# One group's query load, three range checks and a split projection: three moves in the instruction order of a fused linear-attention and SoLU kernel

## The chip, the cores and the metric

The kernel runs on one core of one Trainium2 chip. The metric is device time in microseconds for one launch, lower is better. Three runs of the kernel before are given: 374.28, 375.96 and 377.16 us, median 375.96 us. A further execution was taken with the profiler.

## The reference

A gated linear attention with a per-channel decay is followed by a feed-forward block with a SoLU activation and a layer norm. The attention inputs come as float32, the two weight matrices as float64, and all arithmetic on the chip is float32.

```python
# attention: B, H, S, D = 4, 8, 768, 48; alpha in 0.8 .. 1.0
for t in range(S):
    state = alpha[:, :, t, :, None] * state + k_t (outer) v_t
    y[:, :, t] = q_t @ state
x = y.transpose(0, 2, 1, 3).reshape(B * S, H * D)      # 3072 x 384
h = x @ w_in                                           # 384 -> 1024
solu = h * softmax(h)
ln = (solu - mean(solu)) / sqrt(var(solu) + 1e-6) * g_ln
out = ln @ w_out                                       # 1024 -> 384
```

## The kernel before, in words

The 768 time steps are cut into G = 6 groups of 128. A group holds the 128 steps of all four batches, so the feed-forward block sees 512 token columns per group. For each group the attention part does this:

- `load` brings alpha (`an`), keys (`kn`) and queries (`qn`) from HBM, four requests each on SyncE's queue (SP), one per batch; `load_v` does the same for the values. A queue issues in program order, and a request that has to wait holds up all requests behind it.
- `alpha_T` turns alpha on VectorE, `scan_back` and `scan_on` run the running products of the decay along time on VectorE (L204, three parts each: heads 0 to 3, heads 4 to 7, and the last 16 channels of all heads).
- Keys and queries are multiplied by these products into `kT`, `qv` and `qe`. For group 1 TensorE turns them first (`turned`, L164, tiles `tp_k`, `tp_q`), and VectorE multiplies straight out of PSUM: L779 for the keys, L794 and L802 for the queries.
- `move_lasts` (eight requests, L232) and `move_firsts` (four requests, L237) copy the finished queries within SBUF, from `qe` and `qv` into `q64` (the tile `lot`), which lays two batches on top of each other. These are requests on the same SP queue.
- `scores` (L278) multiplies keys and queries into four PSUM banks `a0` to `a3`, `masked` (L289, VectorE) cuts the upper triangle into `sT`.
- `decay` (L261, GpSimd) multiplies the running `state` by the group's whole decay, which it reads out of the last column of `q64`; then `read_state` (L333, `y<-lot,state`) and `read_values` (L333, `y<-sT,vn`) give the attention output. ScalarE copies it to `x` (L363).
- `up` (L394) gives h in two PSUM buffers `h`; `down` (L507) multiplies the activations by `w_out`. It accumulates eight matmuls in a PSUM buffer `o` per batch, `down(n, half)` giving four of them; a third argument picks some of those four.

Group 0 is special: the weights arrive as float64 words and are rebuilt as float32 on VectorE (`bits`, L612 to L624) while `up` of group 0 runs. `in_range(i)` goes with it: on ScalarE it squares the high words of weight piece i (L598) and takes an exponential of the squares (L601), each with an accumulator read behind it, to find out whether the fast path holds. `alpha_over` (L196) checks the range of alpha in the same manner. The results of both are looked at only at the end of the kernel. `in_range` and `alpha_over` share one scratch tile `sq`. Pieces 5, 6 and 7 lie in slots 1 to 3 of `room`, and the activations of group 1 are written over these slots later.

`mean(0)` sums the columns of `w_out` on TensorE (L645) and ScalarE copies the sums to `o_mean` (L650); `mean(1)` spreads them over the partitions by a matmul (L652) and ScalarE copies that to `mean_sb` (L653). `hold` (L516) copies a finished projection out of PSUM. `finish` does the normalization of one batch and sends it out.

Where the order is written out by hand (the stretch between the end of group 0's `up` and the start of group 1's `up`), each engine executes its instructions in the order of the Python calls. A wait is a semaphore wait at the head of an engine's instruction. This is the stretch that the change touches, from 54 to 104 us of the profile. From group 1's `up` on, the attention of group g+1 is spread over the eight `up` steps of group g by the tables `first` and `usual`; in both tables the queries' load stands behind `move_firsts`.

Of the kernel before, what the change touches and what calls it, by code (L numbers as in the profile page):

```python
# [32 lines left out]
def fast_path(ctx, tc, q, k, v, alpha, moe_w_in, moe_w_out, moe_g_ln, out):  # L33
# [66 lines left out]
    qn = const.tile([P, H, TQ, D], FP, name="qn")  # L100
# [30 lines left out]
    def load(src, dst, g):  # L131
        t = slice(g * P, (g + 1) * P)
        for b in range(B):
            nc.sync.dma_start(
                out=dst[32 * b : 32 * b + 32].rearrange("t h u d -> t h (u d)"),
                in_=src[b, :, t, :].rearrange("h (t u) d -> t h (u d)", u=TQ),
            )
# [20 lines left out]
    def turned(src, ends, out, blocks=range(NB)):  # L158

        x = by_token(src)  # L160
        for j in blocks:
            for b in range(B):
                cols = x[:, b, j, 0:E0] if j < H else ends[:, b, E0 * (j - H) : E0 * (j - H) + E0]
                nc.tensor.matmul(  # L164
                    out[j // NP][32 * b : 32 * b + 32, j % NP], lhsT=cols, rhs=ident, start=True, stop=True,
                    tile_position=(0, 32 * b), skip_group_check=True,
                )
# [10 lines left out]
    def firsts(src, dst):  # L178
        nc.vector.transpose(out=dst.rearrange("p h (t u) -> p h u t", u=TQ), in_=src[:, :, :, 0:E0])  # L179

    def lasts(src, dst):
        nc.vector.transpose(
            out=dst.rearrange("p j (i t u) -> p u j i t", u=TQ, i=2),
            in_=src[:, :, :, E0:D].rearrange("p (j i) u d -> p u j i d", i=2),
        )

    def alpha_T(g):
        nc.gpsimd.memset(aT[:, :, 0:1], 0.0)
        firsts(an, aT[:, 0:H, 1:SW])
        lasts(an, aT[:, H:NB, 1:SW])  # L190

    def alpha_over(g):
        x = an.rearrange("p h u d -> p (h u d)")
        sq = one.tile([P, 768], FP, name="sq").bitcast(U8)[:, 0 : x.shape[1]]
        for i, sign in enumerate((1.0, -1.0)):
            nc.scalar.activation(  # L196
                out=sq, in_=x, func=AF.Relu, scale=sign, bias=mone, accum_out=over[:, g, i : i + 1]
            )
# [28 lines left out]
    def move_lasts():  # L227

        for b in range(B):
            i, c = divmod(b, 2)  # L230
            for k in range(2):
                nc.sync.dma_start(out=q64[64 * i + E0 : 64 * i + 64, c, k::2], in_=qe[32 * b : 32 * b + 32])  # L232

    def move_firsts():
        for b in range(B):
            i, c = divmod(b, 2)
            nc.sync.dma_start(out=q64[64 * i : 64 * i + E0, c], in_=qv[32 * b : 32 * b + 32, 0:H])  # L237
# [27 lines left out]
    def quarter(b):  # L265
        return slice(32 * b, 32 * b + 32)
# [4 lines left out]
    def scores(g, half, a=None):  # L271
        a = a or banks("a", [NP, P])
        for last in range(2):
            for i in (0, 2, 1, 3):
                h = half * NP + i
                kb, qb = (H + h // 2, H + h) if last else (h, h)
                for b in range(B):
                    nc.tensor.matmul(  # L278
                        a[b][:, i], lhsT=kT[quarter(b), kb], rhs=qv[quarter(b), qb, 0:P], start=not last and not i, stop=bool(last),
                        tile_position=(32 * b, 0), skip_group_check=True,  # L280
                    )
        masks[half] = a
# [3 lines left out]
    def masked(half, batches=range(B)):  # L286
        a = masks[half]
        for b in batches:
            nc.vector.tensor_tensor(  # L289
                out=sT[:, b, half * NP : half * NP + NP], in0=a[b], in1=mask[:, None, :].to_broadcast([P, NP, P]),  # L290
                op=ALU.mult,
            )
# [90 lines left out]
    def u_of(g, f):  # L383
        return slots[((0, 5, 4), (1, 2, 3))[g % 2][f // 3]][:, T4 * (f % 3) : T4 * (f % 3) + T4]
# [116 lines left out]
    def down(n, half, part=range(HF)):  # L501
        g, b = divmod(n, B)
        d = st[n]
        if half == 0 and 0 in part:
            d["o"] = ps_o.tile([P, 512], FP, tag="o", name="o")
        for f in (half * HF + i for i in part):
            nc.tensor.matmul(  # L507
                d["o"][:, 0 : DM + 1], lhsT=u_of(g, f)[:, b * P : b * P + P], rhs=w_out[:, f], start=(f == 0),
                stop=(f == FC - 1), skip_group_check=True,
            )  # L510

    def hold(n):

        a = 2 * H * SW + (DM + 1) * (n % 2)
        st[n]["held"] = lot[:, a : a + DM + 1]
        nc.scalar.copy(out=st[n]["held"], in_=st[n]["o"][:, 0 : DM + 1])  # L516
# [73 lines left out]
    def in_range(i, parts=(0, 1)):  # L590


        if not float64:
            return
        if 0 in parts:
            hi = raws[i][:, :, :, 1].bitcast(FP)
            squares[i] = one.tile([P, F], FP, name="sq").rearrange("p (c f) -> p c f", c=hi.shape[1])
            nc.scalar.activation(out=squares[i], in_=hi, func=AF.Square, accum_out=far[:, i, 0:1])  # L598
        if 1 in parts:
            sq = squares.pop(i)  # L600
            nc.scalar.activation(out=sq, in_=sq, func=AF.Exp, scale=-(2.0**24), accum_out=far[:, i, 1:2])  # L601
# [36 lines left out]
    def mean(half):  # L638


        m = ps_h.tile([P, 512], FP, tag="h", name="sums")[:, 0:DM]
        if half == 0:
            for f in range(FC):
                r = quarter(f % 4)
                nc.tensor.matmul(  # L645
                    m[r], lhsT=ones[:, 0:32], rhs=w_out[:, f, 0:DM], start=f < 4, stop=f >= FC - 4,
                    tile_position=(0, r.start), skip_group_check=True,
                )
            made["m"] = work.tile([P, DM], FP, name="o_mean")
            nc.scalar.mul(out=made["m"], in_=m, mul=-1.0 / (32 * DFF))  # L650
        else:
            nc.tensor.matmul(m, lhsT=ones, rhs=made["m"], start=True, stop=True)  # L652
            nc.scalar.copy(out=mean_sb, in_=m)  # L653
# [117 lines left out]
    scaled(7)  # L771
    tq = three("tp_q", [(ps_a, "a0"), (ps_a, "a1")])
    turned(qn, ends_q, tq, range(H))
    in_range(5)
    in_range(6)
    for i in range(3):
        scan_back(1, i)
        part = slice(NP * i, NP * i + NP)
        nc.vector.tensor_tensor(out=kT[:, part], in0=tk[i], in1=hk[:, part], op=ALU.mult)  # L779
    inverses(1)  # L780
    mean(0)
    down(0, 1)
    mean(1)
    hold(0)
    alpha_over(1)
    load(alpha, an, 2)
    tq += three("tp_q2", [(ps_h, "h")])
    turned(qn, ends_q, tq, range(H, NB))
    load(q, qn, 2)
    down(1, 1)  # L790
    hold(1)
    keys_back(1, three("tp", [(ps_a, "a2"), (ps_a, "a3"), (ps_h, "h")]))
# [2 lines left out]
    apart()  # L795
    ends_of_decay()
    move_lasts()
    in_range(7)
    for i in range(2):
        scan_on(1, i)  # L800
        part = slice(NP * i, NP * i + NP)
        nc.vector.tensor_tensor(out=qv[:, part, 0:P], in0=tq[i], in1=aT[:, part, 1:SW], op=ALU.mult)  # L802
    move_firsts()
    down(2, 0)
    scores(1, 0)
    decay(1)
    masked(0)
    alpha_T(2)
    down(2, 1)
    scores(1, 1)  # L810
    masked(1)
# [592 lines left out]
def kernel(tc, *args):  # L1404

    with ExitStack() as ctx:
        taken = fast_path(ctx, tc, *args)
    with tc.If(taken > 0):
        general_path(tc, *args)
# [30 lines left out]
```

## Time and profile before

| what | value |
|---|---|
| median of three runs | 375.96 us (374.28 to 377.16) |
| the profiled execution | 377.03 us |
| its span, first to last instruction | 375.2 us, so 1.83 us lie around it |
| mean granted TensorE clock | 0.995 of full |
| TensorE (PE) busy | 362.3 us, 97% of the span |
| VectorE (DVE) busy | 246.8 us, 66% |
| ScalarE (ACT) busy | 147.0 us, 39% |
| GpSimd (POOL) busy | 125.4 us, 33% |

Each row of the timeline gives the start in us, the length in us, engine, line, operation, the tile written and the tiles read, the size, the number of instructions and, in brackets, the idle time before the first of them with what ended it. Rows of matmuls come in pairs per matmul for float32. TensorE's busy time counts matmuls whose ends are modelled, so 97% says how little it waits, not how well it is used.

The stretches around the change, by busy time of each engine (us in ten us):

| window us | PE | DVE | ACT | POOL | clock |
|---|---|---|---|---|---|
| 60 to 70 | 9.43 | 9.69 | 4.91 | 0.00 | 1.00 |
| 70 to 80 | 8.77 | 9.66 | 8.62 | 0.47 | 1.00 |
| 80 to 90 | 9.52 | 8.00 | 2.09 | 0.00 | 1.00 |
| 90 to 100 | 8.10 | 9.13 | 1.75 | 4.25 | 0.83 |
| 100 to 110 | 10.00 | 9.84 | 7.01 | 4.80 | 1.00 |

### The profile page before, as it was taken

To read this page: it belongs to the slowest core of one execution; us is meant where nothing else is said; L and a number is where in the kernel's file an instruction comes from. 1 tells how busy PE (TensorE), PEld (TensorE's weight loads), DVE (VectorE), ACT (ScalarE), POOL (GpSimd) and SP (SyncE) were. 2 spreads that over 40 slices of the span, in tenths; PEclk is the share of its full clock that TensorE was granted. 3 is DMA by queue.
4 is the path that set the end of the run, shared out by engine and by line. 5 is a ranking of instruction groups with operands and counts; after the bars stand their busy time and mean duration, and the time that the engine had idled before them with its cause. 6 is when DMAs were issued, how large, how long until landed. Compare 5 with 4: busy or idle time off the path is not lost. (4 is left out here: it accounts for less than half of the span.)

```text
span 375.2 us, 10040 instructions
## 1 busy us (share of the span) xinstructions
PE 362.3 (97%) x4341; PEld 216.4 (58%) x4341; DVE 246.8 (66%) x375; ACT 147.0 (39%) x260; POOL 125.4 (33%) x129
## 2 busy tenths in 40 slices
PE   8989999898999999999999999999999999999994
PEld 8775355464755565556575556575555565555652
DVE  1997979979988978954756954756955224544500
ACT  3649853870366253351532251532241231332100
POOL 7020000002347892664112664113673211333200
PEclk9999999999899999999999999999999999999999
DMA  9996986076158706554035354005041000000011
GB/s 179 180 328 158 202 275 134 0 159 124 66 119 178 166 17 132 124 127 113 23 87 106 84 134 107 24 3 107 14 108 35 24 23 0 24 22 21 24 45 49
DMA packets 72871, 36.06 MB, mean 96 GB/s; under 512 B 48232, under 2 KB 70000, under 8 KB 72816
## 3 DMA queue, kind: packets, MB, share of 16 engines
q1 hardware_dynamic: 71792, 34.39, 38.8%
q10 hardware_dynamic: 1024, 0.92, 0.7%
q8 instruction: 36, 0.59, 0.7%
q14 instruction: 19, 0.16, 0.1%
HBM read 25.30 MB, written 4.72 MB: 80 GB/s over the span
## 5 line engine op out<-in xcount | busy, mean ns | idle before, releaser
L507 PE MATMUL o<-w_out,room 128*128 128x385 f32 x384 | 134.9, 496 | 0.0
L394 PE MATMUL h<-x,w_in 128*128 128x512 f32 x288 | 132.2, 599 | 0.6 <-ACT x L363 0.6
L507 PEld LDWEIGHTS o<-w_out,room 128*128 128x128 f32 x384 | 71.6, 191 | 55.0 <-issue 14.4
L394 PEld LDWEIGHTS h<-x,w_in 128*128 128x128 f32 x288 | 52.9, 190 | 58.2 <-issue 48.8
L409 DVE TENSOR_TENSOR room<-h,e 128x512 f32<-128x512 f32 x40 | 27.6, 690 | 61.3 <-ACT e L408 61.2
L408 ACT ACTIVATE e<-h 128x512 f32<-128x512 f32 x40 | 23.8, 596 | 95.8 <-PE h L394 95.5
L427 POOL TENSOR_TENSOR p<-p,e 128x512 f32<-128x512 f32 x30 | 42.9, 1429 | 26.9 <-ACT e L408 26.6
L412 ACT ACTIVATE u<-room 128x512 f32<-128x512 f32 x40 | 25.2, 630 | 36.1 <-DVE room L409 36.1
L546 POOL TENSOR_TENSOR r<-sums,mhalf 128x1 f32<-128x1 f32 x20 | 12.5, 626 | 73.8 <-DVE sums L537 73.8
L289 DVE TENSOR_TENSOR sT<-a,mask 128x512 f32<-128x512 f32 x43 | 26.7, 682 | 13.2 <-PE a L278 13.2
L427 DVE TENSOR_TENSOR p<-p,u 128x512 f32<-128x512 f32 x30 | 24.9, 829 | 7.2 <-ACT u L412 7.2
L204 DVE TENSOR_TENSOR_SCAN hT<-aT,unit 128x516 f32<-128x516 f32 x18 | 23.6, 1356 | 7.6 <-ACT aT L697 7.6
L204 DVE TENSOR_TENSOR_SCAN aT<-aT,seed 128x516 f32<-128x516 f32 x18 | 27.8, 1576 | 0.2
L278 PEld LDWEIGHTS a<-qv,kT 32*128 32x128 f32 x704 | 21.2, 187 | 7.1 <-POOL r L546 1.6
L278 PE MATMUL a<-qv,kT 32*128 32x128 f32 x704 | 23.8, 278 | 0.5 <-DVE qv L802 0.5
L212 POOL COPY fend<-hT 128x12 f32<-128x12 f32 x6 | 4.0, 668 | 59.5 <-DVE hT L204 59.5
L333 PE MATMUL y<-sT,vn 128*32 128x128 f32 x768 | 22.8, 274 | 1.1 <-issue 0.8
L333 PEld LDWEIGHTS y<-sT,vn 128*32 128x32 f32 x768 | 20.7, 110 | 4.4 <-issue 3.8
L225 POOL TENSOR_TENSOR kT<-kT,hT 128x1024 f32<-128x1024 f32 (+1 forms) x8 | 14.2, 1793 | 20.1 <-DVE kT L179 17.8
L196 ACT ACTIVATE sq<-an,mone 128x1536 uint8<-128x1536 f32 x12 | 18.9, 1575 | 0.2
L548 ACT ACTIVATE o_sb<-o,r 128x384 f32<-128x384 f32 x16 | 9.3, 580 | 24.1 <-POOL r L546 24.1
L333 PEld LDWEIGHTS y<-lot,state 64*32 64x32 f32 x640 | 9.5, 108 | 9.6 <-issue 5.8
(148 smaller groups left out, 370.5 us busy)
## 6 DMA issues: line engine op xcount, KB each, us to landing
vn<-in_v_dram SPq DMA_DIRECT2D x24, 192.0 KB, 4.5
an<-in_alpha_dram SPq DMA_DIRECT2D x20, 192.0 KB, 4.2
out_dram<-o_sb SPq DMA_DIRECT2D x20, 192.0 KB, 2.0
room<-in_moe_w_out_dram SPq DMA_DIRECT2D x8, 384.0 KB, 4.6
kn<-in_k_dram SPq DMA_DIRECT2D x16, 192.0 KB, 4.6
qn<-in_q_dram SPq DMA_DIRECT2D x16, 192.0 KB, 4.2
lot<-qe SPq DMA_DIRECT2D x40, 64.5 KB, 2.1
lot<-qv SPq DMA_DIRECT2D x20, 129.0 KB, 2.4
```

The lines of the kernel that those rows point to most:

```text
L196: nc.scalar.activation(out=sq, in_=x, func=AF.Relu, scale=sign, bias=mone, accum_out=over[:, g, i : i + 1])
L204: nc.vector.tensor_tensor_scan(out=o, data0=a, data1=s, initial=1.0, op0=ALU.mult, op1=ALU.add)
L225: nc.gpsimd.tensor_tensor(out=kT[:, part], in0=kT[:, part], in1=hk[:, part], op=ALU.mult)
L278: nc.tensor.matmul(a[b][:, i], lhsT=kT[quarter(b), kb], rhs=qv[quarter(b), qb, 0:P], start=not last and not i, stop=bool(last), tile_posit ...
L289: nc.vector.tensor_tensor(out=sT[:, b, half * NP : half * NP + NP], in0=a[b], in1=mask[:, None, :].to_broadcast([P, NP, P]), op=ALU.mult,)
L333: nc.tensor.matmul(y_bank(b)[quarter(r), a], lhsT=lhsT, rhs=rhs, start=(b, r) not in begun, stop=stop, tile_position=(row, 32 * r), skip_g ...
L394: nc.tensor.matmul(h, lhsT=w_in[:, a, f * P : (f + 1) * P], rhs=d["x"][:, a].rearrange("p b t -> p (b t)"), start=(a == 0), stop=(a == KC ...
L408: nc.scalar.activation(out=e, in_=h, func=AF.Exp)
L409: nc.vector.tensor_tensor(out=u, in0=h, in1=e, op=ALU.mult)
L412: nc.scalar.activation(out=u2, in_=u, func=AF.Square)
L427: eng.tensor_tensor(out=p, in0=d[0][i] if f == 1 else p, in1=d[f][i], op=ALU.add)
L507: nc.tensor.matmul(d["o"][:, 0 : DM + 1], lhsT=u_of(g, f)[:, b * P : b * P + P], rhs=w_out[:, f], start=(f == 0), stop=(f == FC - 1), skip ...
```

## The change

Three moves, all in the hand-written stretch; no operation is added, removed or resized.

1. `load(q, qn, 2)`, the four requests for group 2's queries, moves on SP from ahead of `move_lasts` (eight requests) and `move_firsts` (four) to behind them.
2. `in_range(5)` and `in_range(6)` leave their place ahead of `mean(0)` on ScalarE, `in_range(7)` its place behind `apart`; all three come in one row behind `apart`, which puts the first two behind `alpha_over(1)`, both `hold`s, `keys_back`'s copies and `apart`.
3. `down(0, 1)`, four matmuls between `mean(0)` and `mean(1)` on TensorE, is split: two before `mean(1)`, two behind it.

On VectorE and GpSimd the order of instructions is the same as before. Lines from 774 on are two or three lower in the new file (L779 becomes L777, L794 L792, L802 L799).

```diff
     turned(qn, ends_q, tq, range(H))
-    in_range(5)
-    in_range(6)
     for i in range(3):
         scan_back(1, i)
...
     mean(0)
-    down(0, 1)
+    down(0, 1, (0, 1))
     mean(1)
+    down(0, 1, (2, 3))
     hold(0)
     alpha_over(1)
     load(alpha, an, 2)
     tq += three("tp_q2", [(ps_h, "h")])
     turned(qn, ends_q, tq, range(H, NB))
-    load(q, qn, 2)
     down(1, 1)
     hold(1)
...
     move_lasts()
-    in_range(7)
     for i in range(2):
         scan_on(1, i)
...
     move_firsts()
+    load(q, qn, 2)
     down(2, 0)
     scores(1, 0)
     decay(1)
     masked(0)
     alpha_T(2)
+    for i in range(5, 8):
+        in_range(i)
     down(2, 1)
```

## The prediction

> **What bounds the kernel now.** I read the busy times first, then TensorE's waits, then the timeline of each engine around each wait.
>
> ```profile
> span 375.2 us, 10040 instructions
> PE 362.3 (97%) x4341; PEld 216.4 (58%) x4341; DVE 246.8 (66%) x375; ACT 147.0 (39%) x260; POOL 125.4 (33%) x129
> ```
>
> TensorE has 375.2 - 362.3 = 12.9 us without a matmul in the whole span. Only what shortens these gaps, or TensorE's slow spells, can move the end. The change works between 66 and 94 us; there TensorE waits five times (us in total, times, longest):
>
> ```profile
> PE y L333 <- POOL state L261: 1.7, 1, 1.7
> PE sums L652 <- ACT o_mean L650: 0.7, 1, 0.7
> PE sums L645 <- DVE cols L467: 0.6, 1, 0.6
> PE tp_q L164 <- ACT mean_sb L653: 0.6, 1, 0.6
> PE a L278 <- DVE qv L802: 0.5, 1, 0.5
> ```
>
> The moved range checks stand ahead of the second and fourth, the moved queries ahead of the first. The third and fifth have VectorE behind them, whose order is unchanged. The timeline around the first one:
>
> ```profile
> 76.71 1.79 SPq L134 DMA_DIRECT2D an<-in_alpha_dram  x4
> 78.60 1.87 SPq L134 DMA_DIRECT2D qn<-in_q_dram  x4
> 80.59 6.66 SPq L232 DMA_DIRECT2D lot<-qe  x8
> 87.37 2.77 SPq L237 DMA_DIRECT2D lot<-qv  x4
> ...
> 91.74 2.07 POOL L261 TENSOR_TENSOR state<-state,lot 128x384 f32<-128x384 f32 x2 [16.16 <-DMA lot<-qv]
> ...
> 93.06 0.55 PE L333 MATMUL y<-lot,state 64*32 64x128 f32 x16 [1.66 <-POOL state L261]
> 93.86 1.02 PE L333 MATMUL y<-lot,state 64*32 64x128 f32 x48 [0.25 <-POOL aT L188]
> 94.81 2.86 PE L507 MATMUL o<-w_out,room 128*128 128x385 f32 x4
> 102.65 1.56 PE L507 MATMUL o<-w_out,room 128*128 128x385 f32 x4
> ```
>
> This is a chain: SP issues the query load, then the twelve transfers; GpSimd has been idle for 16.16 us when the last lands and decays the state; TensorE waits 1.66 + 0.25 us. The last two rows show a second price: the same four records take 2.86 us after the stall and 1.56 eight us later. The windows say why (us, then busy time of PE, PEld, DVE, ACT, POOL, granted clock):
>
> ```profile
> 91.43:94.85 3.42, 1.54 (x65) 1.08 (x65) 3.21 (x10) 0.06 (x1) 3.11 (x5) 1.00 0.00 0
> 94.95:98.20 3.25, 3.25 (x28) 1.56 (x36) 2.76 (x3) 1.55 (x3) 0.85 (x2) 0.50 0.34 121
> ```
>
> After 3.42 us in which TensorE was busy for 1.54 (45%), it had half its clock for 3.25 us. That costs 1.6 us more.
>
> **Part 1, the queries behind the transfers.** The first transfer needs `qe`, written by VectorE until 77.98 (L794: 77.29 + 0.69), and SP done with alpha's requests, 78.50 here and about 77.4 with part 2. So it starts near 78.0 instead of 80.59. Eight requests take 6.66 us here, behind two loads, and 5.17 to 5.20 us in the later groups (118.79, 160.19), which have the query load behind them as the change has it. Four more take 2.77. Last issue: 78.0 + 5.2 + 2.8 = 86.0 (87.5 at the slow pace). From the end of issue to GpSimd's start it took 91.74 - 90.14 = 1.60 us here and 1.4 in the next group (127.03 to 128.44). So the decays start at 87.6 (89.1 at worst) and, at 0.84 to 1.26 us each, end by 89.3 to 91.6. TensorE is done with its earlier work at 88.54 + 2.86 = 91.40. The worst case costs 0.2 us, the likely one nothing: I take zero. What is late next is the banks: `masked` frees the last at 88.86 + 2.46 = 91.32. So `read_state` starts at 91.40.
>
> From there to `up` of group 1 TensorE needed 104.05 - 93.06 = 10.99 us. Without half clock and the short stall I take rows of other groups: `read_state` 1.16 twice (133.85, 181.31), two matmuls 1.40 twice, `read_values` 3.65 (99.02 to 102.65): 8.77 us, `up` at 100.2 and 3.85 us earlier.
>
> Not all of it lasts, because VectorE becomes the bound. It runs without a gap from 91.25 to 108, and its chain gets shorter only by what the decays did to it: two one-element instructions took 0.62 and 0.77 us beside them (0.16 elsewhere), and L541 waited 0.63 for ScalarE, which waited for GpSimd's power behind the decays. That is 0.46 + 0.61 + 0.63 = 1.7 us. The first product h times e, at 107.46 now, then comes at 105.7, its `finish(3)` output copy on ScalarE at 107.6 to 108.2 (L548; 109.27 now), and the second exponential stands behind that copy: at 108.2 instead of 111.10, 2.9 us earlier and not 3.85. The rest of that chain, VectorE's transposes and `apart` on ScalarE, ends at 121.31 and TensorE's `scores` of group 2 start at 120.03 with about 0.26 us to spare (the odd heads are read at 121.57). So TensorE keeps 2.9 + 0.26, say 3.1 us. Later TensorE is busy almost throughout (100% in the ten-us windows from 150 on), and what it gains stays.
>
> The query load itself, four requests of 0.45 us, goes out at 86 to 88 and landed 5.4 us after issue: 93. Its reader is the transpose at 115.24, so 22 us cover it. Queued behind it on SP are only outputs, first due at 95.43 and 92.9 after the change. The cover is ample.
>
> **Part 2, the range checks.** Checks 5 and 6, with their accumulator reads, hold ScalarE from 67.18 to 71.19, just ahead of the copy of the sums (L650, at 71.09):
>
> ```profile
> 67.18 0.92 ACT L598 ACTIVATE sq<-room 128x768 f32<-128x768 f32 x1
> ...
> 80.80 0.48 PE L278 MATMUL a<-qv,kT 32*128 32x128 f32 x2
> 81.77 2.06 PE L278 MATMUL a<-qv,kT 32*128 32x128 f32 x62 [0.48 <-DVE qv L802]
> ```
>
> With them gone that copy comes at 68.2 and TensorE's waits of 0.66 and 0.57 us go, 1.23 us. I book none of it. `scores` must not write bank `a1` before VectorE has read `tp_q` out of it, and VectorE is busy without a gap from 55 to 81.71. The wait there grows from 0.48 by 1.23 to 1.7 us, in two pieces: 0.26 for bank `a0` (VectorE until 79.84), then 1.39. Alpha's load comes 1.1 us sooner, which only part 1 uses. At their new place the three checks take 3 x 2.13 = 6.4 us, 80.3 to 86.7; ScalarE then has nothing to do until 92.4 (94.79 now), and the slots they read are rewritten only at 105.7. Cost zero; without that cover each would cost 2.1 us.
>
> **Part 3, the split.** It moves 1.4 us of matmuls behind `mean(1)`, so that they cover ScalarE's copy of 0.48 us that `tp_q` waits for. Its value is inside the 1.23 us and is booked at nothing too.
>
> Sum: 377.03 - 3.1 = 373.9 us for the profiled execution, whose time lies 1.07 above the median. If that lead is the half clock (1.6 us), 373.9 stands as it is; if it is ordinary scatter, the forecast is 375.96 - 3.1 = 372.9. I take the middle, 373.4. If the shown runs mostly had no half clock, the gain against them is only 3.1 - 1.6 = 1.5.
>
> The Trainium skill ("TensorE: Matmul & The Clock Gate", Part 1, and its table of advice) says that half rate comes after a whole idle window of some 3.4 us, counted by a window that runs free. The length fits the 3.25 us here; the threshold does not, since 1.9 us of idling in 3.4 were enough. By the page neither the old stall nor a new one of 1.7 us could halve the clock, and the sum would be 373.9 with no risk; the rows decide, and so the next rival has a price.
>
> **Rivals.** *The new stall halves the clock.* Part 2 gathers 1.65 us of idling before 81.77. If one window holds it all, TensorE is busy for 1.75 of 3.4 us (52%); 45% was too little, and between 71.0 and 74.4 with 1.23 us idle (64%) nothing happened. It sits between, and where the windows lie is chance. Price: 1.6 us on `scores`, which is on the path, hence 373.4 + 1.6 = 375.0.
>
> *More arrives.* If VectorE and ScalarE follow TensorE, all 3.85 us last: 375.96 - 3.85 = 372.1, less with scatter. Against it: the exponential stuck behind the output copy. For it: VectorE idles 1.67 us at 111.73, a reserve.
>
> *Slower.* Half clock at `scores` that lasts for two windows, because slow 32-row matmuls count as little activity: 2 x 1.6 = 3.2 us against 3.1 gained, 377.1 from the profiled time and 1.1 above the median. It decides once the clock stays low beyond 87.7. Against it: in the one spell shown the clock came back after 3.25 us.
>
> *The change does not do what it says:* the transfers are slow because of alpha's bytes, not the queries'. Then they keep 0.83 us per request, the case of 89.1 above, and the stall is still gone but for 0.2 us: inside the forecast.
>
> **How the numbers follow.** Forecast 0.64, half clock at `scores` 0.17, more arrives 0.13, slower 0.06. Range 371.4 (the full 3.85 and 0.7 of scatter, the shown runs lying 1.2 to 1.7 from their median) to 376.2 (half clock and 1.2 of scatter). About one per cent, 3.8 us, is what a measurement of this kernel can tell from no change: below 372.2 lie most of "more arrives" and the edge of the forecast, 0.22; above 379.7 only an unseen mishap, 0.03; between, 0.75.
>
> **What would show it.** Right: transfers issued from 78 to 86, decays ended before 91, no wait of L333 on `state`, clock 1.00 through 95 to 98, range checks on ScalarE from 80 to 87, and the wait for `qv` before `scores` grown to 1.4 us or more while `masked` still starts near 83.7. Wrong: `masked` earlier than 83 (then part 2 pays), a clock below 1.00 behind 81, or TensorE waiting for VectorE's product between 104 and 114.

## The result and the profile after

| | median us | runs | lowest to highest |
|---|---|---|---|
| before | 374.95 | 20 | 373.93 to 377.16 |
| after | 372.82 | 20 | 372.28 to 374.62 |

The ratio is 0.9954 with a 95% interval of 0.994 to 0.9968: the change makes the kernel 0.3 to 0.6% faster, 2.1 us by the medians. The twenty times of the changed kernel lie in two clusters, eleven from 372.28 to 372.88 and nine from 373.98 to 374.62, with nothing between. Each of them has a mean granted TensorE clock: 0.998 to 1.000 in the lower cluster, and 0.992 to 0.995 in eight of the upper nine (0.999 in the ninth, 374.48 us).

The profiled execution of the changed kernel took 374.51 us, its span 372.6. The head of its page and its longest wait of TensorE:

```profile
span 372.6 us, 10040 instructions
PE 361.1 (97%) x4341; PEld 215.8 (58%) x4341; DVE 244.9 (66%) x375; ACT 147.2 (40%) x260; POOL 124.6 (33%) x129
```

```profile
PE a L278 <- DVE qv L799: 1.9, 2, 1.4
```

The wait for the state's decay is no longer among TensorE's waits. In its place stands the wait for bank `a0` and then `a1` before `scores`, 1.9 us instead of 0.5. The timeline after, rows of three engines:

```profile
77.92 5.25 SPq L232 DMA_DIRECT2D lot<-qe  x8
83.28 3.17 SPq L237 DMA_DIRECT2D lot<-qv  x4
86.56 2.30 SPq L134 DMA_DIRECT2D qn<-in_q_dram  x4
...
87.83 1.65 POOL L261 TENSOR_TENSOR state<-state,lot 128x384 f32<-128x384 f32 x2 [12.38 <-DMA lot<-qv]
...
79.77 0.48 PE L278 MATMUL a<-qv,kT 32*128 32x128 f32 x2 [0.54 <-DVE qv L799]
81.64 2.64 PE L278 MATMUL a<-qv,kT 32*128 32x128 f32 x62 [1.38 <-DVE qv L799]
84.21 3.91 PE L507 MATMUL o<-w_out,room 128*128 128x385 f32 x8
...
92.83 1.16 PE L333 MATMUL y<-lot,state 64*32 64x128 f32 x64
```

The transfers go out 2.7 us earlier, the decays begin at 87.83 and are done at 89.48, and `read_state` starts with no wait. But it starts at 92.83 and not at 91.40: the rows of L278 and L507 behind the new wait are longer than elsewhere (62 records in 2.64 us, 2.06 before; eight in 3.91, 2.86 before). The windows of the same profile, columns as in the prediction:

```profile
79.53:82.94 3.41, 1.79 (x46) 1.60 (x50) 2.02 (x3) 3.31 (x8) 0.00 (x0) 1.00 0.67 131
82.94:86.35 3.41, 3.41 (x30) 2.27 (x25) 2.44 (x5) 2.05 (x6) 0.00 (x0) 0.50 0.55 121
```

TensorE was busy for 1.79 of 3.41 us (52%) and then had half its clock for as long. In this profile the spell of half clock has moved from behind the old wait to behind the new one.

### The profile page after: what moved, and what is told of

The parts are those of the page before. It is cut to its first block, busy times and chain, and to the rows that moved or that the text cites. A ratio compares the mean times of both kernels' runs of the same rounds, so it can differ in the third digit from the quotient of the medians.

```text
span 372.6 us, 10040 instructions
## 1 busy us (share of the span) xinstructions
PE 361.1 (97%) x4341; PEld 215.8 (58%) x4341; DVE 244.9 (66%) x375; ACT 147.2 (40%) x260; POOL 124.6 (33%) x129
## 5 line engine op out<-in xcount | busy, mean ns | idle before, releaser
L507 PE MATMUL o<-w_out,room 128*128 128x385 f32 x384 | 134.8, 495 | 0.0
L394 PE MATMUL h<-x,w_in 128*128 128x512 f32 x288 | 132.2, 599 | 0.6 <-ACT x L363 0.6
L507 PEld LDWEIGHTS o<-w_out,room 128*128 128x128 f32 x384 | 71.6, 191 | 55.3 <-issue 14.7
L394 PEld LDWEIGHTS h<-x,w_in 128*128 128x128 f32 x288 | 52.7, 189 | 58.3 <-issue 48.4
L278 PEld LDWEIGHTS a<-qv,kT 32*128 32x128 f32 x704 | 21.9, 189 | 8.8 <-DVE qv L799 2.7
L278 PE MATMUL a<-qv,kT 32*128 32x128 f32 x704 | 24.6, 282 | 2.1 <-DVE qv L799 1.9
L363 ACT COPY x<-y 128x384 f32<-128x384 f32 x24 | 11.2, 479 | 7.3 <-PE y L333 7.1
```

The source lines that it names most:

```text
L278: nc.tensor.matmul(a[b][:, i], lhsT=kT[quarter(b), kb], rhs=qv[quarter(b), qb, 0:P], start=not last and not i, stop=bool(last), tile_posit ...
L394: nc.tensor.matmul(h, lhsT=w_in[:, a, f * P : (f + 1) * P], rhs=d["x"][:, a].rearrange("p b t -> p (b t)"), start=(a == 0), stop=(a == KC ...
L507: nc.tensor.matmul(d["o"][:, 0 : DM + 1], lhsT=u_of(g, f)[:, b * P : b * P + P], rhs=w_out[:, f], start=(f == 0), stop=(f == FC - 1), skip ...
```

## The experiments

Theory A: the query load carries the whole gain; the other two parts only gather TensorE's idling into one wait before `scores`, and that wait halves the clock in some executions. Rival B: the range checks and the split save TensorE about 1.2 us of their own. Rival C: the two clusters come from outside this stretch.

One measure tells most of it apart, since executions differ by up to 1.8 us in when they reach the stretch: S is the start of the sums' matmuls (L645), U the start of `up` of group 1 (L394), both from TensorE's timeline. The last column says whether the clock fell to half between 75 and 100 us. All fourteen profiles, us:

| profile | S | U | U - S | end - U | half clock in 75 to 100 |
|---|---|---|---|---|---|
| before | 66.53 | 104.05 | 37.52 | 271.1 | yes, from 94.9 |
| before_copy | 66.39 | 102.49 | 36.10 | 271.1 | no |
| after | 66.46 | 101.62 | 35.16 | 271.0 | yes, from 82.9 |
| after_copy | 66.09 | 101.19 | 35.10 | 271.0 | yes, from 81.2 |
| after_b | 66.57 | 101.64 | 35.07 | 270.9 | yes, from 82.2 |
| after_c | 66.30 | 99.92 | 33.62 | 271.4 | no |
| after_nosplit | 66.13 | 99.56 | 33.43 | 271.2 | no |
| after_nosplit2 | 66.11 | 99.60 | 33.49 | 272.0 | no |
| q_only | 66.89 | 100.50 | 33.61 | 271.4 | no |
| q_only2 | 67.88 | 102.22 | 34.34 | 270.9 | no |
| checks_split | 67.25 | 102.34 | 35.09 | 271.5 | yes, from 82.2 |
| after_warm | 66.53 | 100.79 | 34.26 | 272.2 | no |
| after_fill | 66.78 | 100.15 | 33.37 | 272.1 | no |
| after_fill2 | 66.25 | 99.79 | 33.54 | 271.9 | no |

Medians are compared on one chip at a time: the kernel before had 375.80 us on the chip of the first four runs, 375.46 on that of the next four and 375.35 on that of the last four. The edits of q_only and q_only2 are shown against the kernel before, all others against the changed kernel.

**q_only: part 1 alone.**

```diff
     turned(qn, ends_q, tq, range(H, NB))
-    load(q, qn, 2)
...
     move_firsts()
+    load(q, qn, 2)
     down(2, 0)
```

> Only the query load is moved; range checks and down(0, 1) stay where they were. Theory A (the query move carries the whole gain; the other two parts only gather TensorE's idling into one stall before scores, and that stall halves the clock in some runs): about 372.5 us in all runs, one cluster, no spell below full clock between 75 and 100 us, TensorE's waits of 0.66 and 0.57 us at the sums back and 0.5 us before scores. Rival B (range checks and split save TensorE about 1.2 us of their own): about 374 us. Rival C (the two clusters of the changed kernel, 372.3 to 372.9 and 374.0 to 374.6, have a cause outside this stretch): two clusters again, 1.7 us apart.

Measured: 373.44 us, ratio 0.9941 (0.9921 to 0.9962), clock 1.00 throughout the stretch. Its timeline:

```profile
78.96 6.41 SPq L232 DMA_DIRECT2D lot<-qe  x8
...
89.32 1.65 POOL L261 TENSOR_TENSOR state<-state,lot 128x384 f32<-128x384 f32 x2 [13.39 <-DMA lot<-qv]
...
82.12 2.06 PE L278 MATMUL a<-qv,kT 32*128 32x128 f32 x62 [0.49 <-DVE qv L801]
...
91.69 1.17 PE L333 MATMUL y<-lot,state 64*32 64x128 f32 x64
```

Here alpha's load comes late, the eight transfers crawl (6.41 us, 0.80 each) and the decays start at 89.32, and still `read_state` at 91.69 waits for nothing. Part 1 alone brings the ratio of all three parts; 2.4 us less than before is short of the expected 372.5, because three of the seven timed runs (374.05 to 374.59) lay apart from four (372.74 to 373.18). The mean clock of all eight runs, the profiled one included, is 0.997 or more, so no half clock at `scores` separates them: part of the scatter comes from elsewhere, as rival C has it. S itself ranges from 66.09 to 67.88 over the profiles.

**q_only2: the same again**, beside the changed kernel.

> The query load alone moved, again, beside the changed kernel on one chip: theory A says no half clock and a median at or below that of the changed kernel; rival B says 0.5 to 1.2 us above it in every run, fast ones compared with fast ones. In the first run three of seven timed runs lay at 374.1 to 374.6, apart from four at 372.7 to 373.2; if that comes back with no half clock in the profile, those clusters have another cause than the wait before scores.

Measured: 373.21 us, ratio 0.9934 (0.9911 to 0.9957), against 373.68 for the changed kernel on that chip; again no half clock in the stretch. Six timed runs lay at 372.75 to 373.24, and the profiled execution alone at 374.89, with S at 67.88 and 0.7 us more between S and U than in q_only, 0.41 of it a gap for which the profile shows no releaser. The mean clock is 0.998 or more in all seven runs. So a late run need not be a run with half clock; that the three late ones of q_only arrived late in the same way is not shown, as none of them was profiled. Rival B falls: without parts 2 and 3 nothing is lost.

**checks_split: parts 2 and 3 without part 1.**

```diff
     turned(qn, ends_q, tq, range(H, NB))
+    load(q, qn, 2)
     down(1, 1)
...
     move_firsts()
-    load(q, qn, 2)
     down(2, 0)
```

> The range checks moved and down(0, 1) split, the query load left in its old place ahead of the transfers. Theory A: TensorE still waits over 1.5 us for the state's decay, the wait before scores is 1.4 us or more, the time is that of the kernel before or worse, 375 to 376.5 us, with up to two spells of half clock. Rival B: about 373.8 us, 1.2 below the kernel before. Rival C says nothing of the median and expects the same spread.

Measured: 374.59 us, ratio 0.9968 (0.9954 to 0.9982), 1.2 us below before. That is rival B's number and not mine. The timeline shows another cause than B's:

```profile
76.12 1.79 SPq L134 DMA_DIRECT2D an<-in_alpha_dram  x4
...
91.64 1.65 POOL L261 TENSOR_TENSOR state<-state,lot 128x384 f32<-128x384 f32 x2 [15.42 <-DMA lot<-qv]
...
82.41 3.58 PE L278 MATMUL a<-qv,kT 32*128 32x128 f32 x62 [1.38 <-DVE qv L800]
...
93.50 1.17 PE L333 MATMUL y<-lot,state 64*32 64x128 f32 x64
```

TensorE saved nothing ahead of `scores`, it waits there for 1.38 us and then has half clock (62 records in 3.58 us). But alpha's load, which stands behind the range check of alpha on ScalarE, went out 1.3 us earlier counted from S (8.87 us after it, 10.18 before), and pulled query load, transfers and decays with it: decays 24.39 us after S, 25.21 before. And TensorE, slowed at `scores`, no longer came early enough to wait for them: the decays end at 93.29 and its earlier work at 93.57. The 0.8 us by which the decays come earlier are most of the 1.2; what makes up the rest is not shown. So parts 2 and 3 are worth something where the query load still blocks the queue; they share their gain with part 1 and do not add to it.

**after_warm: the idling filled with matmuls of ones.**

```diff
     down(2, 0)
+    warm(8, ps_a, "a2")
     scores(1, 0)
```

> The changed kernel with eight more 128x128 matmuls of ones into bank a2 ahead of scores of group 1: added work whose result nobody reads, some 2.3 us, as long as the idling there. Theory A: the slow spell and the upper cluster vanish, all runs between 372.2 and 373.0 us, although work was added; the wait before scores is below 0.3 us. Rival B: no change of the median beyond 0.2 us. Rival C: two clusters as in the changed kernel, median 372.8 or later by what the matmuls add.

Measured: 373.89 us, ratio 0.995 (0.9933 to 0.9967).

```profile
79.13 1.95 PE L452 MATMUL warm<-ones 128*128 128x128 f32 x16
81.01 0.48 PE L278 MATMUL a<-qv,kT 32*128 32x128 f32 x2
81.70 2.06 PE L278 MATMUL a<-qv,kT 32*128 32x128 f32 x62 [0.20 <-DVE qv L799]
...
98.72 0.73 PE L333 MATMUL y<-sT,vn 128*32 128x128 f32 x17 [0.53 <-issue]
```

The half clock is gone as expected, in the profile and by the mean clock of all six runs (0.997 or more), and `scores` takes 2.06 us again. The median is not in the expected band. This execution lost 0.53 us to a gap for which the profile shows no releaser, and 0.67 at the next group's `read_state`. Whether the added work causes them isn't settled by six runs.

**after_fill and after_fill2: the idling filled with half of `down(2, 1)`.**

```diff
     down(2, 0)
+    down(2, 1, (0, 1))
     scores(1, 0)
...
-    down(2, 1)
+    down(2, 1, (2, 3))
     scores(1, 1)
```

> The changed kernel with down(2, 1) split: two of its four matmuls (1.4 us) go ahead of scores of group 1, into the idling. Theory A: idling before scores shrinks to some 0.5 us, no half clock, one cluster at 372.0 to 372.6 us. Two matmuls less now stand between the two scores, so TensorE may wait up to 0.6 us for the banks that masked frees; if VectorE is the bound there, that costs nothing. Rival C: two clusters 1.7 us apart stay.

> The changed kernel with two matmuls of down(2, 1) ahead of scores, again, beside the others on one chip: theory A says one cluster, at the changed kernel's fast cluster or up to 0.3 us below, median about 0.8 us below the changed kernel's if half of that one's runs are slow. Rival C says two clusters.

Measured: 373.02 us, ratio 0.9928 (0.9911 to 0.9945), and 373.43 us, ratio 0.994 (0.992 to 0.996), the second beside 373.68 of the changed kernel. The timeline of the first:

```profile
76.78 4.05 PE L507 MATMUL o<-w_out,room 128*128 128x385 f32 x12
80.77 0.48 PE L278 MATMUL a<-qv,kT 32*128 32x128 f32 x2
81.94 2.06 PE L278 MATMUL a<-qv,kT 32*128 32x128 f32 x62 [0.69 <-DVE qv L799]
...
85.43 3.01 PE L278 MATMUL a<-qv,kT 32*128 32x128 f32 x64
```

The wait is 0.69 us, the clock stays full in both profiles, and U comes 33.4 and 33.5 us after S, little earlier than in after_c, the changed kernel without half clock (33.62): the second `scores` takes 3.01 us instead of 2.07, waiting for the banks as the expectation allowed, and VectorE sets what follows. The timed runs of the second form one cluster 1.1 us wide; in the first, five lie within 0.5 us and the profiled one 0.9 us behind them at 374.04. Of the 0.5 to 0.7 us more behind U than in after_c, 0.56 are a wait for the state's decay in group 2: TensorE arrives earlier than that group's transfers. after_nosplit2 has it too, after_nosplit hasn't, so it isn't the filling's own.

**after_nosplit and after_nosplit2: parts 1 and 2 without part 3.**

```diff
     mean(0)
-    down(0, 1, (0, 1))
+    down(0, 1)
     mean(1)
-    down(0, 1, (2, 3))
     hold(0)
```

> The changed kernel with down(0, 1) whole ahead of mean(1), that is without part 3. The wait of tp_q for the spread sums comes back, some 0.57 us, so the wait before scores shrinks from 1.9 to some 1.3 us in two pieces. Theory A: half clock is rarer than in the changed kernel or gone, since in any window of 3.4 us TensorE is busy for 60% and more; fast cluster at the same time as the changed kernel, because scores starts when VectorE lets it; median equal or up to 0.8 us lower. Rival B (the split itself saves time): about 0.6 us slower in every run.

> The changed kernel without part 3, again: no half clock before 100 us, 33.4 us between those points, median 0.5 to 0.9 us below that of the changed kernel on the same chip. Rival B: at or above the changed kernel.

Measured: 372.82 us, ratio 0.9935 (0.991 to 0.9959), beside 373.68 for the changed kernel; then 373.02 us, ratio 0.9937 (0.9921 to 0.9953), beside 374.24.

```profile
71.76 1.08 PE L164 MATMUL tp_q<-ident,u 128*32 128x128 f32 x32 [0.57 <-ACT mean_sb L653]
...
81.29 2.06 PE L278 MATMUL a<-qv,kT 32*128 32x128 f32 x62 [1.34 <-DVE qv L798]
...
99.56 2.74 PE L394 MATMUL h<-x,w_in 128*128 128x512 f32 x6
```

```profile
79.30:82.70 3.40, 2.06 (x51) 1.71 (x54) 1.90 (x3) 3.30 (x8) 0.00 (x0) 1.00 0.83 164
```

0.57 us of idling is back at `tp_q`, 10 us earlier, and with it out of the window the clock holds: even the 3.4 us with the whole wait in them have TensorE busy for 2.06 us (61%; 60% at least in the second profile). The median is 0.9 and 1.2 us below the changed kernel's. The mean clock is 0.997 or more in all twelve runs, and 0.995 or less in eleven of the 21 runs of the changed kernel beside them; its other ten have medians of 373.16 and 373.12, only 0.1 to 0.3 us above. So part 3 removes a wait and costs time, and nearly all of that cost is the half clock. This version is level with q_only and after_fill within the intervals.

**after_copy, after_b, after_c and before_copy: the two kernels unaltered, for more profiles.**

> The changed kernel unaltered, for a second profile on the chip of the next three. Theory A (its two clusters are the runs with and without a spell of half clock behind the gathered wait before scores of group 1): if the profiled run is of the fast cluster, no spell below full clock between 75 and 100 us although the wait of 1.4 us is there, and up of group 1 begins some 35 us before 135, that is near 100.2; if it is of the slow one, half clock from about 82 to 86 and up near 101.6. Two clusters, some 1.7 us apart. Rival C (clusters from elsewhere): the spell of half clock and the cluster of the run do not go together.

> The changed kernel unaltered, a third profile, beside the version without the split on the same chip. Theory A: from the start of the sums' matmuls (L645) to up of group 1 some 35.1 us when the clock is halved before 87 us, and 33.4 to 33.6 us when it is not; nothing in between. Median of all runs 0.5 to 0.9 us above the version without the split.

> The changed kernel once more, for a profile only: again 35.1 us between those two points with half clock or 33.4 to 33.6 without it. If three or four profiles of four show half clock, it is the rule and not chance.

> The kernel before, a second profile: the wait for the state's decay, some 1.7 us, is there again. If the clock is halved behind it, some 37.5 us between the two points; if it is not, some 35.9 us. The first says that half clock is the usual state of the kernel before, the second that the profile the prediction was made from was a slow draw.

Measured: 373.68 and 374.24 us for the changed kernel, ratios 0.9946 (0.992 to 0.9971) and 0.996 (0.9942 to 0.9978); one execution each of after_c, 373.21, and before_copy, 375.49. Three of four profiles of the changed kernel have half clock and U - S of 35.07 to 35.16; the fourth has neither, with 33.62 us, and its waits before `scores` are the same 0.55 and 1.38 us. The same program with the same idling gets half clock or not, and it is worth 1.5 us between S and U. The kernel before does likewise behind its own wait: 37.52 with, 36.10 without.

The times of after_copy and after_b fill the gap between 372.6 and 375, but the mean clocks sort them. In the nine profiles without the spell the mean is 0.997 to 1.000 and the clock is below full only behind TensorE's last matmul; in the five with it the mean is 0.994 or 0.995. Read so, 19 of all 42 runs of the changed kernel have the spell (0.992 to 0.995, all at 373.98 us or more), and 23 don't (0.998 to 1.000, all but one at 373.68 or less). The clusters are the half clock, but for that one run of 374.48. So rival C falls for the two clusters. Of the kernel before, 15 of the 52 runs beside them lie at 0.995 or less, of checks_split nine of twelve; of the 47 runs of q_only, the fillings and the versions without the split, none.

Why the same waits bring the spell or not can be read from where it begins. The rows of the kernel before around the start of its spell and around the start of the low clock at the end of the kernel, when TensorE has no work left:

```profile
94.80:95.00 0.20, 0.20 (x7) 0.20 (x2) 0.01 (x1) 0.20 (x1) 0.20 (x1) 0.81 0.40 82
374.80:375.00 0.20, 0.00 (x0) 0.00 (x0) 0.00 (x0) 0.00 (x0) 0.00 (x0) 0.54 0.17 41
```

With a clock of either 1 or 0.5, as the longer windows show it, the change lies at 94.92 and 374.82, so 279.89 us apart; read in the same way it is 290.13 in after_copy and 290.14 in checks_split. That is 82, 85 and 85 times 3.413 us, and each of the five spells lasted 3.41 to 3.42. In these executions the clock changes on a grid of 3.413 us. Counted back from the low clock at the end of after_c (from 370.58), the grid cuts the idling before `scores` of after_c in two:

```profile
77.03:80.44 3.41, 2.52 (x9) 1.17 (x7) 3.38 (x4) 2.91 (x6) 0.00 (x0) 1.00 1.02 212
80.44:83.86 3.42, 2.38 (x63) 2.17 (x64) 1.42 (x3) 3.33 (x8) 0.00 (x0) 1.00 0.50 111
```

TensorE is busy for 74 and 70% of these two windows, and for 75 and 71% of the two that share the wait of before_copy (88.70 to 95.53). In after_nosplit the grid cuts the wait as well, so its full clock says little; in after_nosplit2 one window holds all of it (79.44 to 82.86, 2.06 us busy, 60%) and the clock stays full.

## Why the prediction was right, and where it was off

The time, 372.82, is inside the range and on the side forecast. The forecast was a ratio of 373.4 / 375.96 = 0.9932 and 0.9954 was measured: 2.1 us of gain instead of 2.6.

- **Part 1** went as worked out. Transfers from 77.92 to 86.45 (78 to 86 forecast), decays from 87.83 to 89.48 (87.6 to 89.3), no wait at `read_state`, and the queries were issued by 88.86, 24 us ahead of their first reader (113.13). The case of slow transfers was seen too: 6.41 us and decays at 89.32 in q_only (89.1 forecast), still no wait.
- **The 3.85 us at `up`** were right for the profile they were made from: 37.52 - 33.62 = 3.90. Against the kernel before without its half clock it is 36.10 - 33.62 = 2.48, and the prediction's 3.85 - 1.6 = 2.25.
- **What is lost behind `up`** was mis-sized. Forecast was that VectorE and the exponential behind the output copy let 3.1 of 3.85 us through. The chain is there, in the profile of after_c:

```profile
105.13 0.66 DVE L409 TENSOR_TENSOR room<-h,e 128x512 f32<-128x512 f32 x1
...
106.91 0.61 ACT L548 ACTIVATE o_sb<-o_mean,r 128x384 f32<-128x384 f32 x1 [0.45 <-POOL r L546]
107.43 0.58 ACT L408 ACTIVATE e<-h 128x512 f32<-128x512 f32 x1
...
116.16 2.26 PE L278 MATMUL a<-qv,kT 32*128 32x128 f32 x64 [0.20 <-POOL qv L253]
```

The exponential has no idle time ahead of it, it stands behind the copy; but it comes at 107.43 (107.66 with S as before, 108.2 forecast), and `scores` of group 2 at 116.16 instead of 120.03. Behind `up` 271.4 us follow instead of 271.1: 0.3 us lost, not 0.75. Two things were off. VectorE's product came 2.1 us earlier than in the kernel before, counted from S, and not 1.7: the transposes and the scan ahead of it were 0.3 us shorter too, for which I had no term. And VectorE did not become the bound: between 104 and 116 us TensorE's rows show no wait, and the next is the 0.20 us above, for GpSimd's `qv`, which the prediction did not name.

- **Parts 2 and 3 worth nothing** held inside the change: waits of 0.66 and 0.57 us went, and 0.54 + 1.38 us stand before `scores` (0.26 + 1.39 forecast), `masked` starts at 83.91 in the profile with half clock (83.7). The wait grew at the place forecast because VectorE's `qv` sets the start of `scores`: 15.24 us after S before, 15.18 after. The range checks ran from 79.13 to 85.06 in full cover. The remark that only part 1 uses alpha's earlier load was wrong: in checks_split it brings the decays 0.8 us earlier without part 1.
- **The half clock at `scores`** was a rival at 0.17, and a clock below 1.00 behind 81 us was one of the prediction's own signs of being wrong. It came in three of four profiles and, by the mean clocks, in 19 of 42 runs. The step that failed is the chance: I took a window with a busy share of 52% for one that hardly does it. It does: the shares in the windows ahead of the five spells seen are 44 to 52%. That where the windows lie is chance was right. If a spell takes 1.62 us of idling in a window, the least that any of the five had, then with the waits of 0.54 and 1.38 us, 0.48 us apart, 1.6 of the 3.41 us of possible positions give one, 47%; this is an estimate. The price, 1.6 us, was nearly right (1.4 to 1.5 between profiles), and the spell lasts 3.41 us, not 3.25, which was the length of the window that the prediction read.
- **That the half clock did not spoil the forecast is in part luck.** The kernel before has its own spell in 15 of 52 runs and the changed one in 19 of 42, so the medians compare two mixes, and these are not far apart. The eight runs of the changed kernel with the spell, among the twenty, have a median of 374.5. Without the spell the runs of the kernel before have medians of 375.20 and 375.26 on the last two chips, those of the changed kernel 373.16 and 373.12: a gain of 2.0 to 2.1 us, as the profiles say (2.48 - 0.3 = 2.2) and more than the 1.5 that the prediction had for this case.
- For the Trainium skill's page "TensorE: Matmul & The Clock Gate" (Part 1) the measurements decide: the window's length of 3.4 us agrees, and that half rate follows a whole idle window, as its table of the two states has it, falls short, with TensorE busy for 1.5 to 1.8 us of the 3.4 before each spell. That the window runs free agrees with the grid of 3.413 us and with after_c, which has the same waits, cut in two by the grid, and no spell.
- **"More arrives"** is nearly what after_c and after_nosplit are like: U comes 33.4 to 33.6 us after S, and 3.6 of 3.9 us last. The slower rival, half clock for two windows, was not seen: each spell ended after 3.4 us, in after_copy too, where `scores` filled it.

## What to carry to other kernels

On a queue that issues in order, a bulk load whose reader is far off belongs behind the small transfers that somebody is about to wait for; look for the engine that was idle for long when the last one landed. Before removing TensorE's waits, find the wait behind them that someone else sets: what is removed piles up there, and idling in one piece can cost more than the same idling in three, since here the clock was halved by how much of the idling fell into one window of 3.4 us and not by its sum. Compare such versions by a stretch between two instructions of the profile as well as by medians: in the four profiles of the changed kernel the stretch had two values 1.5 us apart, where the medians had scatter. And read the mean clock of every run beside its time: it told which runs had the spell without a profile of each.

## What had not been expected of the hardware

- The clock was halved with TensorE busy for 44 to 52% of the 3.41 us ahead (before 1.61 us, after 1.79, after_copy and after_b 1.49, checks_split 1.68) and was not where the windows around the wait had 60% or more (after_nosplit2 2.06 us, after_c 2.38 and 2.52, before_copy 2.42 and 2.56). Each spell lasted 3.4 us and cost 1.4 to 1.5 us.
- The busy share is not the whole rule. In the first profile of the changed kernel the window of the grid from 366.25 to 369.66, at the end of the kernel, has TensorE busy for 1.51 us (44%), all with 385 columns per matmul, and the clock stays at 1.00 behind it, to the end of the kernel. What makes this window differ from those at `scores` is open.
- The same program reaches the same instruction between 66.09 and 67.88 us after its first one, through gaps in the first 40 us, some of them with no releaser in the profile (0.83 us before 24.89 and 0.64 before 36.69 in q_only2, neither in after_c).
